# Layer norm of the second token block: two one-element steps on ScalarE instead of GpSimd, with a remade instruction order

## The chip, the cores and the metric

The kernel runs on one core of one Trainium2 chip. Its engines work at the same time and meet only at semaphores: TensorE (PE, matmuls), VectorE (DVE), ScalarE (ACT), GpSimd (POOL), and SyncE (SP), which here issues nearly all DMA transfers. The metric is the device time of one execution in microseconds (us). "Before" is the median of four runs.

## The reference

A two-layer MLP over 2048 tokens behind a layer norm without learned scale or shift. Everything arrives and leaves in bfloat16.

```python
B, S, D, F = 1, 2048, 1024, 3584
def _layernorm(x, axis=-1, eps=1e-5):
    m = jnp.mean(x, axis=axis, keepdims=True)
    v = jnp.var(x, axis=axis, keepdims=True)
    return (x - m) / jnp.sqrt(v + eps)

def reference(x, w1, b1, w2, b2):
    y = _layernorm(x, axis=-1)
    h = _gelu(jnp.einsum("bsd,df->bsf", y, w1) + b1)
    return jnp.einsum("bsf,fd->bsd", h, w2) + b2
```

`_gelu` is the tanh approximation.

## The kernel before, in words

**Blocks and products.** The tokens are worked in two blocks of 1024 (`NSB` = 2, `s` = 0 and 1), each of eight tiles of 128. For each block the kernel normalises the tiles, forms the first product and the Gelu (`mm1_unit`, `mm1_group`, `mm1_plain`), then the second product (`mm2_block`). Both products are cut in two along each dimension and done in seven half-size products instead of eight, with additions before and after them; some of these halves are cut once more (`inner`, `mm1_group`). So PE needs fewer matmuls, and VectorE has many sums to make: sums of operands in SBUF (line 854 and others), and sums of a PSUM bank and a saved copy of it (`plus`, recorded at line 942, and lines 807 and 821). ScalarE copies PSUM banks to other banks or to SBUF (lines 780 and 962) and does the Gelus (line 792). A product that accumulates on such a copy can't start before the copy is done.

**Block 0's head.** The first tiles of x are loaded, normalised with statistics on VectorE or ScalarE (`ln`, `ln_act`), transposed on PE (line 504), and multiplied as soon as they are there (`mm1_plain`, line 619). Meanwhile PE runs 26 matmuls on ones (line 400). The bias b1 comes as rows and is transposed by one small matmul (`b1t`, line 406); its copy `b1c` is read by every Gelu.

**Block 1's layer norm.** It is `ln_act2`, line 464, and runs during block 0: three tiles (6, 7, 3) while block 0's first product runs, and five (0, 1, 2, 4, 5) while its second product does. For a tile ScalarE sums x into an accumulator (`sum`, line 469), scales the sum to the negative mean (`nm`, line 472), and squares x with that mean as bias into another accumulator (`sq`, line 474). GpSimd then makes variance plus epsilon (`vpe`, line 482), raises it to the power -1/2 (`rstd`, line 485), and multiplies negative mean and `rstd` for the bias (`nb`, line 488). Last, ScalarE writes the normalised tile as `x * rstd + nb` (`y`, line 491). Two transposing transfers per tile (`dma_T`, line 520) bring it into the layout of the first product. `vpe`, `rstd` and `nb` have one element per partition.

**What sets the order.** Each operation is given to a planner (`Planner`) with its engine, an assumed duration, the operations it depends on and a priority. The planner plays the engines forward in time and takes, on each, among those that can start soonest the one of smallest priority; the result is each engine's fixed instruction order. `ORDER` is a table that shifts the priorities of named operations. `LAT` and `PE_LAT` are assumed delays between engines. `_emit` writes each engine's instructions in that order and puts a semaphore wait ahead of an instruction for each dependence not yet known as met. This includes an engine's own earlier instructions, except for PE, which is given no wait for itself. An engine works strictly in its order: a waiting instruction holds all that stand behind it, and so does a waiting transfer on SP's queue.

**Buffers of the second product.** Within `last_block`, the four sums of an inner product on its left side (`s1` to `s4` in `inner`) go to buffers used again two products later. `war_of` lists what must be done before such a buffer is written anew: the matmuls that read it (`subs`), and stores that read it. That `s2` reads `s1`, and `s4` reads `s2`, on the same engine, is not in the list. `o22` at the end of `last_block` is made in two VectorE sums.

Of the kernel before, what the change touches and what calls it, by code (L numbers as in the profile page):

```python
# [5 lines left out]
ACT = mybir.ActivationFunctionType  # L6
ALU = mybir.AluOpType
BF16 = mybir.dt.bfloat16
FP16 = mybir.dt.float16
F32 = mybir.dt.float32  # L10
# [12 lines left out]
LN_EPS = 1e-5  # L23
P = 128
# [12 lines left out]
DMA_T = (5, 6, 7)  # L37

ORDER = {n: float(x) for n, x in (e.split(":") for e in """
    G1_5g_0_5:5.5 G1_5g_1_5:8.8 G2_5g_0_3:-15.8 G2_5g_1_3:0.8 G3_5g_0_3:7.3 G3_5g_0_5:-4.7 G3_5g_1_1:-25.3  # L40
    G4_5g_1_1:13 G6_5g_0_5:-21 G7_5g_0_3:9.2 G7_5g_0_5:6.5 M11_1:8.3 M15_0:17 M24_0:-3.1 M27_1:5.7 M43_0:-8.5
    M47_0:7.7 M51_1:7.2 M57_0:16.8 M6_0_0:3.3 M72_1:-20.2 O12_0_1:11.2 O12_0_3:8.4 P1_0_6:10.3 P1_0_9:-1.1
    P1_1_2:-2.7 P1_1_3:-18.7 P1_1_6:0.2 P2_0_12:-1 P2_0_5:0.7 P3_0_10:-9.9 P3_0_11:5.1 P3_0_12:-7.3 P3_0_2:-10.3
    P3_1_6:9.8 P4_0_3:7.4 P4_0_9:-17.7 P4_1_0:40.5 P4_1_1:54.4 P4_1_3:2 P6_0_12:-3.6 P6_0_4:1.1 P6_1_11:4.1
    P7_0_6:-33.7 c7_0_11:2.3 c7_0_5:1.2 c7_0_8:-5.5 c7_0_9:8.4 c7_1_12:9.1 c7_1_13:1.2 g12_1_1:13.1 g12_1_3:2.2
    g21_1_8:25.8 g22_0_2:1.3 g22_0_3:1.6 gS0_5g_1_3:20 gS1_5g_0_3:-6.6 gS1_5g_0_5:11.2 gS3_5g_0_5:14.9 g_0_3_2:-14.6
    hS2_0_1:-7.5 hS3_1_0:8.3 hS4_0_1:-4.8 hS4_0_3:39 iS3_1_1_0:41 iS3_2_0_0:8.3 iS5_3_1_0:28.6 iS5_4_0_0:-14.1
    iS5_5_0_0:-10 iS6_5_0_0:-3.7 iT4_1_0_0:4.1 iT4_2_0_0:3.8 iT4_3_0_0:13.3 iT5_3_0_0:14.2 iT6_1_0_0:4.6
    iT6_2_0_0:1.3 iT6_4_0_0:6.6 iT6_5_0_0:-8.9 k5_3_1:16.7 k5_5g_0_5:35.6 o12_3_0:-17 pT1_2:-34.8 pT1_3:15 pT1_6:4.8
    pT2_1:1.7 pT2_2:7.7 pT3_3:10.8 pT3_5:-2.2 pT4_0:-7.2 pT4_3:-4.3 pT4_4:-7 pT4_5:-2.4 pT4_6:7.9 plain_0_7_2None:35  # L50
    plain_0_7_3None:8.5 pw2_0:-4.4 r11_5g_1_5:-18.2 r12_5_0:10.8 r22_1_0:14.3 r22_5g_0_3:33.7 s2_2_0:-7.2
    sd1_0_2:11.5 sn1_0_9:12.1 sn1_1_10:2.8 sn1_1_5:-0.5 sn5_0_4:-29.1 st0_5_0:-3.9 w1T13_1_0:3.4 w1T1_0_4:30.1
    w1T1_0_6:-5.1 w1T1_1_2:3.5 w1T2_1_1:26.1 w1T3_0_6:-17.7 w1T4_1_3:15 w1_0_0_1:9.9 w1_0_3_0:-7.9 w1_0_5_0:-24
    w1_0_5_1:-0.6 w1_1_0_0:0.7 w1_1_6_1:-1.9 w6_0_11:-4.1 w6_0_5:-9.5 w6_1_5:-44.2 wi5_3:20.8 x0_0_1:-11.2 x1_0:4.8
    y1_6:-8.5 yS1_1_0:6.2 yS2_0_0:8.2 yS2_1_0:-3.4 yS4_1_0:8.6 yi13_1:14.5 yi2_0:-15 yt0_6_0:-2.3
""".split())}

MM512 = 0.2159
MM256 = 0.1092
MM128 = 0.0562  # L60
LAT = 0.12
PE_LAT = 0.2
DMA_RATE = 0.35e6
DMA_RATE0 = 0.29e6
# [41 lines left out]
class Planner:  # L106
# [8 lines left out]
    def add(self, *a, **k):  # L115
        o = Op(*a, **k)
        o.prio += ORDER.get(o.name, 0.0)
        self.ops.append(o)
        return o
# [29 lines left out]
    def place(self):  # L149
        free = {e: 0.0 for e in self.ENGS}  # L150
# [11 lines left out]
        while left:  # L162
# [32 lines left out]
                o.deps += list(dict.fromkeys(rel for rel in rels if rel is not None))  # L195
                h.pool.free = [f for f in h.pool.free if not k <= f[0] < k + h.n]
            c = o.cost[e] if isinstance(o.cost, dict) else o.cost
            free[e] = r + c
            if o.nbytes is not None:
                dma_free = max(dma_free, r + c)  # L200
                dma_free += o.nbytes / (DMA_RATE0 if dma_free < 4.0 else DMA_RATE)
# [57 lines left out]
def bass_standalone__mixer_channel_mlp__prompt_kernel(  # L259
# [24 lines left out]
    with ExitStack() as es:  # L284
# [18 lines left out]
        identb = sb("identb", [P, P], BF16)  # L303
        ones = sb("ones", [P, P], FP16)
        nhalf = sb("nhalf", [P, 1], F32)
        st_sb = sb("st_sb", [P, NT, 12], F32)
        mv_sb = sb("mv_sb", [P, NT, 2], F32)
        vpe_sb = sb("vpe_sb", [P, NT], F32)
# [59 lines left out]
        def load_w1(s, c, prio, gate=(), eng="SP"):  # L368
# [11 lines left out]
                                                           compare_op=ALU.is_equal, fill=0.0, base=0,  # L380
                                                           channel_multiplier=1), (c_ones,), -7, "identb")
        c_nh = add("POOL", 0.1, lambda e: e.memset(nhalf[:, :], -0.5), (), -8, "nhalf")

        load_x(0, 0, (), -400, halves=True, eng=("SP", "ACT"))
        load_x(0, 1, (), -390)
# [12 lines left out]
        def warm(n, deps, prio):  # L398
# [5 lines left out]
        warm(N_WARM, (), -200)  # L404
        hold_b = Holder(banks, leaves=False)
        b1t = add("PE", 0.2, [(lambda e: e.transpose(out=ps16[:, hold_b.k, 0:FT].bitcast(BF16), in_=b1r_sb[:, :],
                                                    identity=identb[0:FT, 0:FT]), ())], (c_idb, b1_ld), 11.0, "b1t",
                  alloc=hold_b)
        b1c = add("ACT", 0.2, lambda e: e.copy(out=b1_sb[:, :], in_=ps16[:, hold_b.k, 0:FT].bitcast(BF16)), (b1t,), 12.0,
                  "b1c", frees=(hold_b,))  # L410
# [53 lines left out]
        def ln_act2(s, i, prio, war=None):  # L464


            junk = junk1 if war is None else junk2
            war = [*(war or ()), *junk_last[-1:]]
            a0 = add("ACT", 1.25, lambda e: e.activation(out=junk, in_=x_sb[:, i, :].rearrange("p (a c) -> p a c", a=2), func=ACT.Identity,  # L469
                                                         accum_out=mv_sb[:, i, 0:1]), [*x_ld[(s, i)], *war], prio,  # L470
                     f"sum{s}_{i}")
            a1 = add("ACT", 0.2, lambda e: e.mul(mv_sb[:, i, 1:2], mv_sb[:, i, 0:1], -1.0 / D), (a0,), prio + 0.001,
                     f"nm{s}_{i}")
            a2 = add("ACT", 1.35, lambda e: e.activation(out=junk, in_=x_sb[:, i, :].rearrange("p (a c) -> p a c", a=2), func=ACT.Square,  # L474
                                                         bias=mv_sb[:, i, 1:2], scale=1.0,
                                                         accum_out=st_sb[:, i, 0:1]), (a1,), prio + 0.002,
                     f"sq{s}_{i}")
            junk_last.append(a2)
            if junk is junk1:
                for u in (NU - 2, NU - 1):  # L480
                    h_head.setdefault((22, u), []).append(a2)
            vp = add("POOL", 0.2, lambda e: e.tensor_scalar(out=vpe_sb[:, i:i + 1], in0=st_sb[:, i, 0:1],
                                                           scalar1=1.0 / D, scalar2=LN_EPS, op0=ALU.mult, op1=ALU.add),
                     (a2,), prio + 0.003, f"vpe{s}_{i}")
            rs = add("POOL", 0.6, lambda e: e.tensor_tensor(out=rstd_sb[:, i:i + 1], in0=vpe_sb[:, i:i + 1],
                                                            in1=nhalf[:, :], op=ALU.pow), (vp, c_nh), prio + 0.004,
                     f"rstd{s}_{i}")
            nb = add("POOL", 0.3, lambda e: e.tensor_tensor(out=st_sb[:, i, 1:2], in0=mv_sb[:, i, 1:2],  # L488
                                                            in1=rstd_sb[:, i:i + 1], op=ALU.mult), (rs, a1), prio + 0.005,
                     f"nb{s}_{i}")  # L490
            y_ok[(s, i)] = add("ACT", 1.3, lambda e: e.activation(  # L491
                out=x16[:, i, :], in_=x_sb[:, i, :], func=ACT.Identity, scale=rstd_sb[:, i:i + 1],
                bias=st_sb[:, i, 1:2]), (nb, rs), prio + (0.006 if war is not None else 6.0), f"y{s}_{i}")
# [112 lines left out]
        def mm1_plain(c, prio):  # L606
# [3 lines left out]
            for b in range(2):  # L610
                hold = [Holder(banks) for _ in range(4)]
                done = {f: [] for f in range(4)}
                for i in range(b * TH, (b + 1) * TH):
                    t = i % TH
                    y = y_in[(0, i)]
                    for j, f in ([(j, f) for j in range(2) for f in range(4)] if i == 0 else
# [4 lines left out]
                            rhs=yop[f"A{b + 1}{k // KH + 1}"][:, k % KH, t * P:(t + 1) * P],  # L621
                            start=(k == t == 0), stop=(k == KD - 1), skip_group_check=True),
                            (ld[k // KH], y[k // KH])) for k in ks]
                        o = add("PE", len(ks) * MM128, fn, list(dict.fromkeys([*done[f][:1]] + [d for _, dd in fn for d in dd])),
                                prio[i] + 0.01 * f + 0.1 * (j or 0), f"plain_{c}_{i}_{f}{j}",
                                alloc=hold[f] if t == 0 and not j else None)
                        w1_use[c].append(o)
# [301 lines left out]
        def mm2_block(s, W):  # L929
# [8 lines left out]
            kept = {p: [] for p in SEQ2}  # L938
            stores = []
            last_ = {}  # L940
            done = lambda p: users[p]
            plus = lambda e, out, x, y: e.tensor_tensor(out=out, in0=x, in1=y, op=ALU.add)  # L942

# [92 lines left out]
            def inner(p, a, Yo, xb, war, O=None, bias=None, out=None, gate=(), ogate=(), kk=None, tmp=None, tail=False):  # L1036
# [19 lines left out]
                    Holder(banks, seeded=bias is not None)  # L1056
                bank = {1: c0, 6: c0, 7: c0, 4: c0, 2: c2, 5: c5, 3: c5}
                subs, ev = {}, {}

                def sub(r, deps, alloc=None):  # L1060
                    x, y = opn[r]
# [122 lines left out]
            def last_block():  # L1184
# [39 lines left out]
                def give(names, subs):  # L1224
                    for r, b in zip(SEQ1, names):
                        use[b] = [subs[r]]
# [38 lines left out]

                gw, okq, sub7 = inner(7, S3, Yo[7], XX, war_of(sub2), O=(g1, O12), kk=dl_sb[:, :], gate=(sub5[5],))
                give(hold[7], sub7)
                for i in range(2):
                    ho = Holder(outs, 2)
                    q = 10 * i + 11  # L1270
                    rows = lambda g, i=i: sn_sb[:, g.k + 2 * i:g.k + 2 * i + 2, :].rearrange(
                        "p j (v c) -> p v j c", v=2)
                    f = [add("DVE", 1.22, lambda e, i=i, ho=ho, rows=rows: plus(
                        e, o_sb[:, ho.k:ho.k + 2, :].rearrange("p v (j c) -> p v j c", j=2), rows(gw), rows(g5)),
                        (okq[q], okq[q + 1], *O12.values()), pt[7] + 7 * SUB + 0.1 * i, f"o22_{s}_{i}", alloc=ho,
                        frees=(g5,) if i else ())]
                    store(22, 2 * i, 2, ho, f, pt[7] + 7 * SUB)

# [2 lines left out]
                      tail=True)  # L1281

            def war_of(subs, p=None):
                return {(c, r): [subs[r]] + ([ti_st[p][r]] if c == "T" and r in ti_st.get(p, {}) else [])
                        for c in "ST" for r in subs}

            if s + 1 == NSB:
# [225 lines left out]
```

## Time and profile before

| what | us |
|---|---|
| median of four runs | 338.58 (338.35 to 339.25) |
| the profiled execution's own time | 338.51 |
| its span, first to last instruction | 336.8 |
| PE busy | 330.4 |
| VectorE busy | 281.6 |
| ScalarE busy | 173.4 |
| GpSimd busy | 22.3 |
| ScalarE waiting for GpSimd's `nb` (line 488), 4 times | 6.7 |

The span leaves out what lies before the first and after the last instruction. Matmuls are pipelined: a matmul's recorded length is longer than the distance to the next start, and rows of busy time hide gaps that are shorter than that difference. The distance between starts is the better measure. An engine's idle time costs nothing unless something on the path that ends last waits for it. GpSimd's lengths include the time in which it waits for SBUF.

### The profile page before, as it was taken

How to read it: one execution, taken by the hardware profiler on the slowest of the kernel's cores; microseconds unless marked ns; L12 is line 12 of the kernel's file. 1: busy time of each engine (PE TensorE's matmuls, PEld its weight loads, DVE VectorE, ACT ScalarE, POOL GpSimd, SP SyncE). 2: the span in 40 equal slices, each digit the busy share in tenths (PEclk: the TensorE clock that was granted, in tenths of full speed). 3: DMA queues.
4: the chain of work that ended last, by engine and by line, in shares of the span. 5: the costliest groups of instructions: out<-in, count | busy, mean ns of one | idle time of the engine just before them, and what ended most of it. 6: DMA issues, size and time to landing. Idle time of an engine off the chain costs nothing.

```text
span 336.8 us, 6035 instructions
## 1 busy us (share of the span) xinstructions
PE 330.4 (98%) x2399; PEld 224.2 (67%) x2399; DVE 281.6 (84%) x381; ACT 173.4 (52%) x292; POOL 22.3 (7%) x47
## 2 busy tenths in 40 slices
PE   5999999999999999999999999999999999999996
PEld 4977445445468885547875555544545888888885
DVE  3986789998999989979999978886738879999984
ACT  5675878566876687612113666765675521010200
POOL 2320120000020413200000000000000000000000
PEclk9999999999999999999999999999999999999999
DMA  7896999797879999899859549839972999998103
GB/s 220 281 204 164 357 364 307 262 305 255 270 279 275 362 356 360 221 295 373 345 174 313 185 187 333 291 130 293 350 233 54 385 313 365 333 366 274 64 0 127
DMA packets 80310, 89.47 MB, mean 266 GB/s; under 512 B 15130, under 2 KB 67226, under 8 KB 79770
## 3 DMA queue, kind: packets, MB, share of 16 engines
q1 hardware_dynamic: 80138, 88.95, 81.8%
q8 instruction: 19, 0.31, 0.4%
q10 hardware_dynamic: 144, 0.13, 0.1%
q14 instruction: 9, 0.07, 0.1%
HBM read 61.81 MB, written 24.38 MB: 256 GB/s over the span
## 4 chain that ended last, share of the span: by engine, by line
PE 93%; ACT 3%; DMA 2%; POOL 1%; issue 0%; SPq 0%; DVE 0%
PE ps L767 42%; PE ps L1063 34%; PE ps L978 7%; PE ps L619 5%; PE ps L692 5%; DMA w_sb<-in_w_dram 2%; POOL st_sb L488 1%; ACT t_sb L474 1%; PE ps L504 1%; ACT t_sb L469 1%; PE ps L1068 0%; ACT sn_sb L962 0%; ACT ps L962 0%; ACT x_sb L491 0%; SPq L350 0%
## 5 line engine op out<-in xcount | busy, mean ns | idle before, releaser
L767 PE MATMUL ps<-yw_sb,t_sb 128*128 128x512 f16 x336 | 80.0, 379 | 0.0
L767 PE MATMUL ps<-yw_sb,w_sb 128*128 128x512 f16 x312 | 74.7, 379 | 0.0
L792 ACT ACTIVATE h_sb<-ps,b_sb 128x512 f16<-128x512 f32 x78 | 52.9, 687 | 37.0 <-PE ps L767 32.3
L767 PEld LDWEIGHTS ps<-yw_sb,t_sb 128*128 128x128 f16 x336 | 32.7, 98 | 35.9 <-DVE ps L807 0.5
L767 PEld LDWEIGHTS ps<-yw_sb,w_sb 128*128 128x128 bf16 x312 | 30.3, 98 | 33.2 <-ACT ps L780 0.3
L854 DVE TENSOR_TENSOR h_sb<-h_sb 128x2048 f16<-128x2048 f16 (+2 forms) x36 | 38.6, 1085 | 7.3 <-ACT h_sb L792 5.3
L962 ACT COPY sn_sb<-ps 128x512 f32<-128x512 f32 x27 | 15.5, 584 | 32.9 <-DVE o_sb L942 18.2
L1063 PE MATMUL ps<-w2a_sb,h_sb 128*128 128x256 f16 (+1 forms) x252 | 30.3, 273 | 0.0
L942 DVE TENSOR_TENSOR sn_sb<-ps,sn_sb 128x512 f32<-128x512 f32 x35 | 24.0, 688 | 5.3 <-PE ps L1063 4.5
L1063 PEld LDWEIGHTS ps<-w2a_sb,h_sb 128*128 128x128 f16 x252 | 24.7, 98 | 3.9
L942 DVE TENSOR_TENSOR o_sb<-ps,sn_sb 128x512 bf16<-128x512 f32 (+1 forms) x29 | 19.3, 670 | 6.3 <-PE ps L1063 3.7
L978 PE MATMUL ps<-w2a_sb,h_sb 128*128 128x512 f16 x112 | 24.5, 379 | 0.0
L1063 PE MATMUL ps<-w_sb,t_sb 128*128 128x256 f16 x196 | 23.4, 273 | 0.1
L962 ACT COPY ps<-sn_sb 128x512 f32<-128x512 f32 x12 | 7.1, 589 | 30.3 <-PE ps L1063 24.6
L780 ACT COPY ps<-ps 128x512 f32<-128x512 f32 x26 | 14.9, 577 | 14.5 <-PE ps L767 14.5
L1063 PEld LDWEIGHTS ps<-w_sb,t_sb 128*128 128x128 f16 x196 | 19.0, 98 | 2.7 <-ACT sn_sb L962 0.4
L807 DVE TENSOR_TENSOR ps<-ps,sn_sb 128x512 f32<-128x512 f32 x26 | 17.7, 695 | 3.5 <-PE ps L767 3.4
L587 DVE TENSOR_TENSOR t_sb<-w_sb,t_sb 128x1024 f16<-128x1024 bf16 x26 | 17.9, 688 | 3.2 <-DMA w_sb<-in_w_dram 2.0
L792 ACT ACTIVATE h_sb<-sn_sb,b_sb 128x512 f16<-128x512 f32 x26 | 18.5, 717 | 3.7 <-DVE sn_sb L821 2.8
L978 PEld LDWEIGHTS ps<-w2a_sb,h_sb 128*128 128x128 f16 x112 | 11.0, 98 | 12.8
L619 PE MATMUL ps<-yw_sb,w_sb 128*128 128x128 f16 x256 | 17.4, 231 | 0.3 <-DMA w_sb<-in_w_dram 0.3
L821 DVE TENSOR_TENSOR sn_sb<-ps,sn_sb 128x512 f32<-128x512 f32 x20 | 13.6, 688 | 4.5 <-PE ps L767 4.4
(125 smaller groups left out, 486.8 us busy)
## 6 DMA issues: line engine op xcount, KB each, us to landing
w_sb<-in_w_dram SPq DMA_DIRECT2D x28, 512.0 KB, 5.9
x_sb<-in_w_dram SPq DMA_DIRECT2D x21, 256.0 KB, 6.2
w_sums<-x_sb SPq DMA_DIRECT2D x21, 256.0 KB, 3.5
w2a_sb<-w_inner_sums SPq DMA_DIRECT2D x12, 448.0 KB, 7.2
x_sb<-in_x_dram SPq DMA_DIRECT2D x15, 256.0 KB, 6.1
w_inner_sums<-w_sb SPq DMA_DIRECT2D x4, 896.0 KB, 8.7
x_sb<-w_sums SPq DMA_DIRECT2D x2, 1792.0 KB, 8.9
w_sb<-w_inner_sums SPq DMA_DIRECT2D x8, 448.0 KB, 7.2
```

Of the source, the lines that this page charges most:

```text
L587: return add("DVE", 0.65, lambda e: e.tensor_tensor(out=tv(k), in0=x0, in1=x1, op=ALU.subtract), [*deps, *war.get(k, ())], prio + 0.5 * k, ...
L619: fn = [(lambda e, b=b, hb=hold[f], f=f, k=k, t=t: e.matmul(ps[:, hb.k, t * P:(t + 1) * P], lhsT=lhs[:, k, f * P:(f + 1) * P], rhs=yop[f"A ...
L692: fn = [(lambda e, k=k, v=v: e.matmul(ps[:, bank[r].k, v * QN:(v + 1) * QN], lhsT=xo()[:, k, v * P:(v + 1) * P], rhs=yv()[:, k, :], start= ...
L767: fn = [(lambda e, k=k: e.matmul(ps[:, hold[p].k, :], lhsT=lhs[:, k, :], rhs=yop[yo][:, k, :], start=(first and k == 0), stop=(k == KH - 1 ...
L780: return e.copy(out=dst, in_=src) if o_.eng == "ACT" else e.tensor_copy(dst, src)
L792: r = h_ok[(s, q, u)] = add("ACT", 0.70, lambda e: e.activation(out=dst, in_=src(), func=ACT.Gelu_apprx_tanh, bias=b1_sb[:, f:f + 1], scal ...
L807: o2 = add("DVE", 0.7, lambda e: e.tensor_tensor(out=b5v(b5), in0=b5v(b0), in1=v5(), op=ALU.add), (P6, *o5), pt[7] - SLOT, f"w6_{nm}", all ...
L854: o = add("DVE", cost2(w * dst.shape[-1]), lambda e, k0=k0, k1=k1: e.tensor_tensor(out=dst[:, k0:k1, :], in0=a[0][:, k0:k1, :], in1=b[0][: ...
L942: plus = lambda e, out, x, y: e.tensor_tensor(out=out, in0=x, in1=y, op=ALU.add)
L962: return act(lambda e: e.copy(out=out(), in_=src()), deps, at - 5, name, **k)
L978: fn = [(lambda e, k=k, t=t: e.matmul(ps[:, banks_[t].k, :], lhsT=a[0][:, k, t * P:(t + 1) * P], rhs=b[0][:, k, :], start=(first and k == ...
L1063: fn = [(lambda e, k=k, j=j: e.matmul(ps[:, bank[r].k, j * HI:(j + 1) * HI], lhsT=x[0][:, k, j * P:(j + 1) * P], rhs=y[0][:, k, :], start= ...
```

## The change

In `ln_act2`, `vpe` becomes a ScalarE activation (Identity, scale 1/D, bias from a new one-column tile `epsc` that holds epsilon), and `nb` becomes a ScalarE multiply with a per-partition scale. `rstd` stays on GpSimd, now planned at 2.0 us instead of 0.6. For the three early tiles `nb` gets a priority 6 higher. A GpSimd memset fills `epsc`.

The planner subtracts 0.08 us from each VectorE and 0.09 us from each ScalarE operation when it works out when the engine is free (`OVL`). The bias transpose `b1t` moves from priority 11 to -92, and the plain products of the second half of the tiles depend on it. `war_of` now also lists the left-side sums that read `s1` and `s2`, and the second `o22` sum depends on the first. The table `ORDER` is remade: some entries stay, many are dropped, changed or new. Of it only a few lines are shown.

```diff
 ORDER = {n: float(x) for n, x in (e.split(":") for e in """
-    G1_5g_0_5:5.5 G1_5g_1_5:8.8 G2_5g_0_3:-15.8 G2_5g_1_3:0.8 G3_5g_0_3:7.3 G3_5g_0_5:-4.7 G3_5g_1_1:-25.3
+    G1_5g_0_5:5.5 G1_5g_1_3:2 G1_5g_1_5:-3 G2_5g_0_3:-15.8 G2_5g_1_3:4.3 G2_5g_1_5:-2.9 G3_5g_0_3:8.5
...
-    y1_6:-8.5 yS1_1_0:6.2 yS2_0_0:8.2 yS2_1_0:-3.4 yS4_1_0:8.6 yi13_1:14.5 yi2_0:-15 yt0_6_0:-2.3
+    yS1_1_0:3.6 yS2_0_0:8.2 yS4_1_0:9.1 yi13_1:15.1 yi2_1:-4.4 yi4_1:-1.5
 """.split())}
...
+OVL = {"DVE": 0.08, "ACT": 0.09}
...
-            free[e] = r + c
+            free[e] = r + c - OVL.get(e, 0.0)
...
+        epsc = sb("epsc", [P, 1], F32)
...
+        c_eps = add("POOL", 0.1, lambda e: e.memset(epsc[:, :], LN_EPS), (), -6, "eps")
...
-                                                    identity=identb[0:FT, 0:FT]), ())], (c_idb, b1_ld), 11.0, "b1t",
+                                                    identity=identb[0:FT, 0:FT]), ())], (c_idb, b1_ld), -92.0, "b1t",
...
-            vp = add("POOL", 0.2, lambda e: e.tensor_scalar(out=vpe_sb[:, i:i + 1], in0=st_sb[:, i, 0:1],
-                                                           scalar1=1.0 / D, scalar2=LN_EPS, op0=ALU.mult, op1=ALU.add),
-                     (a2,), prio + 0.003, f"vpe{s}_{i}")
-            rs = add("POOL", 0.6, lambda e: e.tensor_tensor(out=rstd_sb[:, i:i + 1], in0=vpe_sb[:, i:i + 1],
+            vp = add("ACT", 0.2, lambda e: e.activation(out=vpe_sb[:, i:i + 1], in_=st_sb[:, i, 0:1], func=ACT.Identity,
+                                                        bias=epsc[:, :], scale=1.0 / D), (a2, c_eps), prio + 0.003,
+                     f"vpe{s}_{i}")
+            rs = add("POOL", 2.0, lambda e: e.tensor_tensor(out=rstd_sb[:, i:i + 1], in0=vpe_sb[:, i:i + 1],
                                                             in1=nhalf[:, :], op=ALU.pow), (vp, c_nh), prio + 0.004,
                      f"rstd{s}_{i}")
-            nb = add("POOL", 0.3, lambda e: e.tensor_tensor(out=st_sb[:, i, 1:2], in0=mv_sb[:, i, 1:2],
-                                                            in1=rstd_sb[:, i:i + 1], op=ALU.mult), (rs, a1), prio + 0.005,
-                     f"nb{s}_{i}")
+            nb = add("ACT", 0.2, lambda e: e.mul(st_sb[:, i, 1:2], mv_sb[:, i, 1:2], rstd_sb[:, i:i + 1]), (rs, a1),
+                     prio + (0.005 if war is not None else 6.0), f"nb{s}_{i}")
...
-                        o = add("PE", len(ks) * MM128, fn, list(dict.fromkeys([*done[f][:1]] + [d for _, dd in fn for d in dd])),
+                        o = add("PE", len(ks) * MM128, fn, list(dict.fromkeys([*done[f][:1], *([b1t] if b else [])] + [d for _, dd in fn for d in dd])),
...
+            s_read = {}
...
+                s_read[id(subs)] = {5: s2[1][0], 6: s4[1][0]}
...
+                f = []
...
-                        (okq[q], okq[q + 1], *O12.values()), pt[7] + 7 * SUB + 0.1 * i, f"o22_{s}_{i}", alloc=ho,
+                        (okq[q], okq[q + 1], *O12.values(), *f), pt[7] + 7 * SUB + 0.1 * i, f"o22_{s}_{i}", alloc=ho,
...
-                return {(c, r): [subs[r]] + ([ti_st[p][r]] if c == "T" and r in ti_st.get(p, {}) else [])
+                return {(c, r): [subs[r]] + ([ti_st[p][r]] if c == "T" and r in ti_st.get(p, {}) else []) + (
+                    s_read[id(subs)].get(r, []) if c == "S" else [])
```

More of the change, by code (lines that the diff above doesn't have):

```diff
@@ L39 @@
 ORDER = {n: float(x) for n, x in (e.split(":") for e in """
-    G1_5g_0_5:5.5 G1_5g_1_5:8.8 G2_5g_0_3:-15.8 G2_5g_1_3:0.8 G3_5g_0_3:7.3 G3_5g_0_5:-4.7 G3_5g_1_1:-25.3
-    G4_5g_1_1:13 G6_5g_0_5:-21 G7_5g_0_3:9.2 G7_5g_0_5:6.5 M11_1:8.3 M15_0:17 M24_0:-3.1 M27_1:5.7 M43_0:-8.5
-    M47_0:7.7 M51_1:7.2 M57_0:16.8 M6_0_0:3.3 M72_1:-20.2 O12_0_1:11.2 O12_0_3:8.4 P1_0_6:10.3 P1_0_9:-1.1
-    P1_1_2:-2.7 P1_1_3:-18.7 P1_1_6:0.2 P2_0_12:-1 P2_0_5:0.7 P3_0_10:-9.9 P3_0_11:5.1 P3_0_12:-7.3 P3_0_2:-10.3
@@ L44 @@
[L44 to L53, printed above, removed]
@@ L54 @@
-    w1_0_5_1:-0.6 w1_1_0_0:0.7 w1_1_6_1:-1.9 w6_0_11:-4.1 w6_0_5:-9.5 w6_1_5:-44.2 wi5_3:20.8 x0_0_1:-11.2 x1_0:4.8
-    y1_6:-8.5 yS1_1_0:6.2 yS2_0_0:8.2 yS2_1_0:-3.4 yS4_1_0:8.6 yi13_1:14.5 yi2_0:-15 yt0_6_0:-2.3
+    G1_5g_0_5:5.5 G1_5g_1_3:2 G1_5g_1_5:-3 G2_5g_0_3:-15.8 G2_5g_1_3:4.3 G2_5g_1_5:-2.9 G3_5g_0_3:8.5
+    G3_5g_1_1:-37.6 G5_5g_0_3:5.9 G7_5g_0_3:9.2 M11_1:7 M12_1:-22 M23_0:-5.1 M27_1:5.7 M35_0:-3.3 M42_0:-4.6
+    M45_0:16.6 M47_0:7.7 M47_1:-10.4 M51_1:7.2 M52_1:-3.3 M57_0:16.8 M72_1:-20.2 P1_0_6:-3.7 P1_0_9:-1.1 P1_1_2:-4
@@ new lines @@
+    P1_1_3:-25.5 P1_1_9:-0.9 P2_0_8:9 P2_0_9:1.3 P2_1_6:6.6 P2_1_9:4.5 P3_0_11:5.1 P3_0_12:-7.3 P3_0_2:-2.5
+    P3_0_6:-18.5 P3_1_1:-7 P3_1_3:12.1 P3_1_5:2.1 P3_1_6:9.8 P3_1_7:0.4 P4_0_3:7.3 P4_0_4:2.4 P4_0_7:5.1 P4_1_0:29.5
+    P4_1_1:54.9 P6_0_13:3.3 P6_0_8:-3.6 P6_1_9:-7.6 P7_0_6:-34.1 P7_0_9:-5.2 P7_1_4:2.7 c7_0_8:-32.2 c7_0_9:7.5
+    c7_1_12:9.1 c7_1_2:21.7 c7_1_3:-7.4 g22_1_1:-37.4 g22_1_4:-5.7 gS1_5g_0_3:-17.2 gS3_5g_0_5:17.1 gS3_5g_1_1:-0.3
+    hS2_0_2:-4.4 iS3_2_0_0:9.2 iS5_3_1_0:28.6 iT4_3_0_0:13.3 iT57_4_0:-17.9 iT57_5_0:-10.6 iT6_1_0_0:4.6
@@ new lines @@
+    iT6_3_0_0:1.5 k5_3_1:16.7 pT1_3:31.6 pT2_1:-33.5 pT2_2:7.5 pT2_3:7.7 pT3_3:11.5 pT3_5:4.4 pT3_6:-4.5 pT4_0:-16.5
+    pT4_4:-6.6 pT4_6:8.9 plain_0_7_2None:35 pw2_0:-6.6 r22_1_0:23.5 sn1_0_12:3.7 sn1_1_7:-6.2 sn1_1_8:-2.4
+    sn5_0_4:-29.1 st0_4_1:11.2 tI7_3:32.2 tl6:-16.4 w1T13_1_0:-15.3 w1T1_0_4:29.4 w1T2_1_1:17.3 w1T3_0_6:-16.9
+    w1T4_1_0:15.9 w1_0_0_1:9.9 w1_0_5_0:-24 w1_1_2_0:0.4 w1_1_4_1:-36.8 w1_1_6_1:-4.8 w2_0_B22_1:2 w6_0_6:1.7
+    w6_0_7:7.6 w6_1_0:-2.9 w6_1_3:20.1 w6_1_4:-0.3 w6_1_5:-47.2 x0_0_1:-11.2 x1_0:4.8 y0_1:14.5 y1_6:-8.5
```

## The prediction

> **What bounds the kernel now.** I read the share table first. In these rows each engine has its busy time, its share of the span and its instructions.
>
> ```profile
> span 336.8 us, 6035 instructions
> PE 330.4 (98%) x2399; PEld 224.2 (67%) x2399; DVE 281.6 (84%) x381; ACT 173.4 (52%) x292; POOL 22.3 (7%) x47
> PEclk9999999999999999999999999999999999999999
> ```
>
> TensorE (PE) has work for 98% of the span at full clock, and the change touches none of its 2399 matmuls. The question is only how much idle time is in the other 2%, and whether the change can reach it. The chain that ended last, in order of time (start, length, what), shows where PE is not the releaser:
>
> ```profile
> 1.73 5.91 DMA w_sb<-in_w_dram
> 7.69 1.89 PE ps L619 x16
> ...
> 19.95 1.79 PE ps L619 x32
> ...
> 113.09 0.76 POOL vpe_sb L482
> ...
> 114.54 2.83 POOL st_sb L488
> 117.38 0.03 issue
> 117.40 1.24 ACT x_sb L491
> ...
> 122.54 4.76 PE ps L1063 x42
> ...
> 154.53 18.34 PE ps L1063 x168
> ...
> 332.70 1.54 PE ps L1068 x14
> 334.25 0.02 issue
> 334.27 0.42 DVE o_sb L942
> ```
>
> Up to 7.69 the first weights arrive; from 334.25 the last sum and store run out (2.5 us); between, PE. At 108.7 to 122.5 the chain wanders over ScalarE and GpSimd (ACT and POOL), 13.8 us long. That is not 13.8 us of stall: the table by stretches has PE busy for 14.00 of the 14.00 us from 108 to 122. The timeline tells what was lost. Columns: start, length, engine, line, operation.
>
> ```profile
> 114.30 2.02 DVE L1022 TENSOR_TENSOR w_sb<-yw_sb 128x3584 f16<-128x3584 bf16 x1
> 114.54 2.82 POOL L488 TENSOR_TENSOR st_sb<-mv_sb,rstd_sb 128x1 f32<-128x1 f32 x1
> 116.23 1.09 DVE L854 TENSOR_TENSOR t_sb<-h_sb 128x1792 f16<-128x1792 f16 x1
> 117.40 1.24 ACT L491 ACTIVATE x_sb<-x_sb,st_sb,rstd_sb 128x1024 f16<-128x1024 bf16 x1 [2.00 <-POOL st_sb L488]
> 118.55 0.56 ACT L962 COPY sn_sb<-ps 128x512 f32<-128x512 f32 x1
> 121.92 0.56 ACT L962 COPY sn_sb<-ps 128x512 f32<-128x512 f32 x1
> 122.53 1.42 PEld L1063 LDWEIGHTS ps<-w_sb,t_sb 128*128 128x128 f16 x14 [0.40 <-ACT sn_sb L962]
> ```
>
> A one-element GpSimd multiply took 2.82 us, until two VectorE (DVE) sums had ended. ScalarE stood 2.00 us before the normalising activation, so everything behind it in ScalarE's order came late. The PSUM copy that ended at 122.48 held PE: the matmul starts around it are 0.395 us apart where 0.109 is usual, so 0.286 us were lost. It is the only such gap between 12 and 334 us.
>
> Matmul starts give the rest. From 7.69 on, spacing above the usual is 2.51 us in all: 0.286 here; 0.191 and 0.106 in the head, around the bias transpose at 9.51; 1.77 is early 128-column matmuls spaced 0.107 instead of 0.056; the last 0.15 is scatter.
>
> **What the Trainium skill says.** "GPSIMD Engine Reference", section "Key points": GpSimd contends for SBUF with a VectorE instruction that has two SBUF inputs. The trace agrees: L488 took 0.19 us with a PSUM-reading sum beside it, and 2.82, 1.23, 1.05 and 1.02 us beside two-SBUF-input sums. "ScalarE: Activation LUTs", section "What ACT_TABLE_LOAD costs": an ACTIVATE costs 186 ns, plus 93 for each per-partition pointer operand, and back-to-back ones overlap by 93 ns. The trace has 200 ns for the 128x1 one without pointers (L472), and copies of 0.56 to 0.59 us start 0.48 us apart. "TensorE: Matmul & The Clock Gate", section "Part 1: The HAM clock gate": a cold array runs at half clock until it has been busy for one free-running window. That fits the 0.107 spacing up to 12.07 us, which this edit cannot shorten by design, though its end can move between executions.
>
> **The change part by part.**
>
> *Removed from GpSimd.* Eight variance steps (L482, 3.0 us in all, mean 372 ns) and eight bias steps (L488, 7.2 us, mean 897). ScalarE waited 6.7 us in four stalls for the latter. What of that is on PE's path is the 0.286 us.
>
> *Added to ScalarE.* Eight variance activations with one pointer (the epsilon column) and eight multiplies scaled by a pointer. No such row exists with pointers; nearest is L472 at 0.200, and the skill's price is 0.28. I take 0.28, bounds 0.20 and 0.37. Then 16 x 0.28 = 4.5 us, 5 x 0.56 = 2.8 of it between 108 and 142 us, where the stalls saved were four, 6.7 us. ScalarE is busy 10.42 of 14 us from 108 to 122 and 14.43 of 23 from 122 to 145; 3.6 and 8.6 us are free, so the extra is hidden if the order keeps it out from before a copy that PE waits for. Uncovered, one pair is 0.56 us against copy margins down to 0.09 us: the copy that starts at 118.55 ends at 119.11, and the matmul that needs it starts at 119.20. That would be a stall of about 0.5 us.
>
> *The chain of one tile.* Before, worst case: square ends 113.00, normalising starts 117.40, 4.4 us. After: variance 0.28 + hop 0.07 + power 0.56 + hop 0.06 + bias 0.28 + 0.03 = 1.3 us plus whatever holds the power.
>
> *The power that stays.* L485 took 0.55 us in seven of eight cases, because the variance step ahead of it absorbed the hold (0.74, 0.70, 0.45, 0.32 us where 0.19 is free). It will now be first at the port. Holds seen on a first step average 0.18 us; on any step the longest is 2.82 - 0.19 = 2.63. I take 0.2 to 0.5, bounds 0 and 2.63. The order table assumes 2.0 us for it, so up to 1.45 us of hold has other ScalarE work planned over it.
>
> *Transposes.* The normalised tiles leave by two transposing transfers each on SP's queue (118.67 and 120.85 for this tile). They are unchanged in number but become free up to 2 us sooner; behind them in that queue stand loads of w2 sums, which can only be released earlier by it. Worth nothing on PE, whose gaps here are not transfers.
>
> *Epsilon memset.* One more on GpSimd, 0.10 us like L382, at about 1.65 us; the engine is idle from there to 5.18. Free.
>
> *Bias transpose.* Its priority rises, and second-half plain matmuls name it as an earlier step on PE, for which PE emits no wait. It already ran at 9.51, when nothing else was ready. I take 0 with bounds -0.3 (both head gaps close) and +0.3.
>
> *Own-engine order.* New waits on VectorE for its own earlier work: the next sums' buffers wait for sums several instructions back, met long ago; the second of two closing sums waits for the first, losing an overlap of about 0.08 us (sums of 0.69 start 0.61 apart). VectorE is busy 28.06 of 30 us from 290 to 320, but these come where PE is several products ahead. 0, upper bound 0.3.
>
> *The order table.* The largest unknown. Every engine's order is made anew, with VectorE and ScalarE operations counted 0.08 and 0.09 shorter, which are the overlaps the trace shows. The old order leaves PE one gap in 322 us. A new one can hardly do better, and any product put before its copy or sum is late costs a gap: margins at PE's waits, from the end of the copy or sum to the matmul that needs it, start at 0.09 us, and many are 0.6 to 0.8. I take +0.1, bounds 0 and +3 (several sums late by one 0.69 us place).
>
> Sum for the likeliest: -0.286 + 0 + 0 + 0.1 = -0.2 us. The profiled execution took 338.51 (span 336.8, 1.7 around it), the median 338.58, 0.07 more. So 338.51 - 0.2 + 0.07 = 338.4.
>
> The floor follows too. With all of 0.286, 0.191, 0.106 and the scatter of 0.15 gone the gain is 0.73 us, 337.85. Only a half-clock phase that ends sooner goes below: 1.77 us at the very most.
>
> **The rivals.** *A: no measurable change, 338.4*, as summed. For it: one matmul order is as dense as another once operands are in time. Against: new orders rarely meet every margin.
>
> *B: slower, the new order opens gaps in PE, 339.6.* Mechanism: a VectorE sum that is read by the next product (L807 and L942 in the two matrix products) takes a place behind an operand sum of 1.09 us. VectorE has only 16% free, so it cannot catch up at once. With a usual margin of 0.64 us each such place costs 1.09 - 0.08 - 0.64 = 0.37 us; four give 1.5, less 0.29 saved: 338.58 + 1.2 = 339.8, three give 339.4. It decides from three places on. Against: the durations assumed now fit the trace better than before.
>
> *C: slower by the power's hold, 339.3.* At a tile whose power meets two long sums (2.63 us, as L488 did), ScalarE stands at the bias step 1.2 us past the plan, and the PSUM copy behind it has 0.09 to 0.8 us of margin: 0.4 to 1.1 us a time. Two such tiles near 1.0 less 0.29 give 339.3; one alone stays within A. Against: the first-step holds seen end at 0.55 us.
>
> *D: faster, 337.7.* The gap at 122.5 and the head's gaps close, and the half-clock phase ends a little sooner. For it: four holds of GpSimd go. Against: only 0.73 us is there without the clock.
>
> That the change doesn't do what it says is unlikely: its functions are Identity and a scaled copy, and Identity (L469) already runs between Gelus with a single table load in the whole profile.
>
> **How the numbers follow.** A 0.46, B 0.28, C 0.09, D 0.17. 0.2% of 338.58 is 0.68 us, about what a measurement of this kernel can tell from no change; so A lies within, B and C above 339.26, D below 337.90: faster 0.17, same 0.46, slower 0.37. A's own range is 337.9 to 339.2. For 8 in 10, D's best third is left out below and the upper third of B above: 337.6 to 340.6.
>
> **What would show it.** Right: L482 and the bias line appear on ScalarE near 0.2 to 0.3 us each; GpSimd keeps only L485 in block 1, with one or two held above 1 us; ScalarE's 6.7 us of waits for GpSimd shrink to under 3; PE's start gap at 122.5 is gone; the head to 7.69 and the tail of 2.5 us stay. A wrong forecast would show as start gaps on PE over 0.3 us: beside a late VectorE sum it is B, beside a copy behind the bias step C. A head whose half-clock spacing ends elsewhere than 12 us would mean the clock, not the edit, moved the time.

## The result, and the profile after

The changed kernel takes 340.06 us in the median (338.69 to 346.50, 33 executions), the kernel before 338.63 (337.46 to 340.28, 52). The ratio is 1.0048, with a 95% interval of 1.0036 to 1.0059: about 1.6 us slower. (The ratios leave out disturbed executions, so they are not exactly the quotients of the medians.)

The profiled execution hides this. It took 338.69 us, the fastest of all 33, and its span, 336.9 us, is that of the execution profiled before (336.8). First the share table:

```profile
span 336.9 us, 6019 instructions
PE 329.9 (98%) x2399; PEld 223.6 (66%) x2399; DVE 278.7 (83%) x380; ACT 178.0 (53%) x309; POOL 15.0 (4%) x32
```

The groups of the moved steps (busy and mean length; then the idle time before them):

```profile
L483 ACT ACTIVATE vpe_sb<-st_sb,epsc 128x1 f32<-128x1 f32 x8 | 2.3, 292 | 0.2
L486 POOL TENSOR_TENSOR rstd_sb<-vpe_sb,nhalf 128x1 f32<-128x1 f32 x8 | 6.9, 864 | 112.6 <-ACT vpe_sb L483 112.6
L489 ACT ACTIVATE st_sb<-mv_sb,rstd_sb 128x1 f32<-128x1 f32 x8 | 2.3, 289 | 1.6 <-POOL rstd_sb L486 1.6
```

The move did what it says. The two steps cost 0.29 us each on ScalarE; GpSimd has 7.3 us less work; ScalarE waits 1.6 us for GpSimd instead of 6.7. The power now takes the wait that GpSimd's first step has beside VectorE's sums: 0.86 us in the mean instead of 0.57. The gap of 0.286 us at 122.5 us is gone.

But PE has new gaps, in the head. From PE's timeline of the changed kernel (idle time and releaser in brackets; the recorded length hides part of a gap):

```profile
16.85 0.62 PE L504 MATMUL ps<-ident,x_sb 128*128 128x128 f16 x8 [0.26 <-DVE x_sb L430]
23.08 1.89 PE L767 MATMUL ps<-yw_sb,w_sb 128*128 128x512 f16 x8
25.21 1.99 PE L619 MATMUL ps<-yw_sb,w_sb 128*128 128x128 f16 x28 [0.24 <-DMA yw_sb<-x_sb]
```

By the distance between starts, 0.42 us are lost at 16.85, where tile 4's normalising (L430) is late, and 0.40 and 0.24 us at 25.21 and 25.68, where the plain products of tile 6 wait for its two transposed halves.

The first of these is no late load: tile 4 had landed at 10.01. In the remade order its normalising stands on VectorE behind tile 5's and behind a sum of weights (L587), and it waits for a GpSimd power that took 0.86 us beside that sum, where the one before it took 0.57:

```profile
15.10 0.69 DVE L587 TENSOR_TENSOR t_sb<-w_sb 128x1024 f16<-128x1024 bf16 x1
15.35 0.86 POOL L427 TENSOR_TENSOR rstd_sb<-vpe_sb,nhalf 128x1 f32<-128x1 f32 x1
16.25 0.55 DVE L430 TENSOR_SCALAR x_sb<-x_sb,mv_sb,rstd_sb 128x1024 f16<-128x1024 bf16 x1 [0.46 <-POOL rstd_sb L427]
```

For the gaps of tile 6, SP's queue shows what stands in front of its transposes. Before:

```profile
16.11 0.93 SPq L350 DMA_DIRECT2D w_sb<-in_w_dram  x2
17.42 8.39 SPq L520 DMA_TRANSPOSE yw_sb<-x_sb  x6
```

After:

```profile
15.21 2.62 SPq L520 DMA_TRANSPOSE yw_sb<-x_sb  x2
17.88 1.14 SPq L350 DMA_DIRECT2D w_sb<-in_w_dram  x2
19.47 5.88 SPq L520 DMA_TRANSPOSE yw_sb<-x_sb  x4
```

A megabyte of weights now stands between tile 5's and tile 6's transposes. It landed at 24.68 us, tile 6's halves at 25.16 and 25.64. Before, PE came to tile 6 only at 26.81, 2.0 us after the second half had landed.

From PE's first transpose on, start gaps over 0.07 us add up to 1.89 us, 1.80 of them before 26 us; before it was 1.13. That is 0.76 more. But the early half-clock spacing (0.107 us between matmuls of 128 columns instead of 0.056) ended sooner, at 11.07 us against 12.21 (the prediction read 12.07), so it and the scatter came to 1.69 us instead of 2.43, which is 0.74 less. The two cancel, and the span is nearly the same. The half-clock phase ended anywhere from 9.5 to 14.6 us in the profiles that follow.

### The profile page after: what moved, and what is told of

It reads as the page before. It is cut to its first block, busy times and chain, and to the rows that moved or that the text cites. A ratio compares the mean times of both kernels' runs of the same rounds, so it can differ in the third digit from the quotient of the medians.

```text
span 336.9 us, 6019 instructions
## 1 busy us (share of the span) xinstructions
PE 329.9 (98%) x2399; PEld 223.6 (66%) x2399; DVE 278.7 (83%) x380; ACT 178.0 (53%) x309; POOL 15.0 (4%) x32
## 4 chain that ended last, share of the span: by engine, by line
PE 92%; DVE 4%; DMA 2%; POOL 1%; issue 0%; SPq 0%; DVEq 0%
PE ps L767 41%; PE ps L1065 38%; PE ps L979 7%; PE ps L692 5%; DVE st_sb L419 2%; DMA yw_sb<-x_sb 1%; PE ps L619 1%; DMA x_sb<-in_x_dram 1%; DVE x_sb L430 1%; POOL rstd_sb L427 1%; PE ps L1070 0%; DVE mv_sb L423 0%; DVE x_sb L453 0%; DVE yw_sb L511 0%; POOL vpe_sb L424 0%
## 5 line engine op out<-in xcount | busy, mean ns | idle before, releaser
L767 PEld LDWEIGHTS ps<-yw_sb,w_sb 128*128 128x128 bf16 x312 | 30.4, 98 | 33.1
L943 DVE TENSOR_TENSOR sn_sb<-ps,sn_sb 128x512 f32<-128x512 f32 x35 | 23.8, 686 | 1.5 <-PE ps L1065 1.4
L587 DVE TENSOR_TENSOR t_sb<-w_sb,t_sb 128x1024 f16<-128x1024 bf16 x26 | 17.8, 684 | 3.4 <-PE ps L767 2.3
L619 PEld LDWEIGHTS ps<-yw_sb,w_sb 128*128 128x128 bf16 x256 | 15.7, 102 | 2.0 <-DMA yw_sb<-x_sb 1.0
```

Of the source, the lines that this page charges most:

```text
L587: return add("DVE", 0.65, lambda e: e.tensor_tensor(out=tv(k), in0=x0, in1=x1, op=ALU.subtract), [*deps, *war.get(k, ())], prio + 0.5 * k, ...
L619: fn = [(lambda e, b=b, hb=hold[f], f=f, k=k, t=t: e.matmul(ps[:, hb.k, t * P:(t + 1) * P], lhsT=lhs[:, k, f * P:(f + 1) * P], rhs=yop[f"A ...
L767: fn = [(lambda e, k=k: e.matmul(ps[:, hold[p].k, :], lhsT=lhs[:, k, :], rhs=yop[yo][:, k, :], start=(first and k == 0), stop=(k == KH - 1 ...
```

## The experiments

After the result there were two theories, not to be mixed up with the prediction's rivals A to D: **theory A**, the remade order costs the time (in the head, or in the body, which here means all after 30 us), and **theory B**, the two steps on ScalarE cost it. A start gap is the amount by which the distance between two matmul starts exceeds the usual one.

| kernel | median us | ratio to before | 95% interval |
|---|---|---|---|
| changed, again | 340.16 | 1.0048 | 1.0029 to 1.0068 |
| changed, again | 340.28 | 1.0044 | 1.0016 to 1.0072 |
| new order, steps on GpSimd | 340.97 | 1.0069 | 1.0037 to 1.0100 |
| kernel before, steps on ScalarE | 338.24 | 0.9989 | 0.9973 to 1.0004 |
| all of the change but the order | 338.52 | 0.9984 | 0.9971 to 0.9996 |
| the same, again | 338.34 | 0.9987 | 0.9974 to 0.9999 |
| old head, new rest | 339.19 | 1.0014 | 0.9992 to 1.0036 |
| the same, again | 339.55 | 1.0019 | 1.0003 to 1.0035 |
| new head, old rest | 340.74 | 1.0059 | 1.0037 to 1.0081 |
| old to 95 us, new after | 339.23 | 1.0011 | 0.9997 to 1.0025 |
| new from 30 to 95 us only | 339.74 | 1.0026 | 1.0008 to 1.0043 |

**Order against operations.** The first two experiments take the steps and the order apart. In one, the changed kernel keeps its order and the steps go back to GpSimd around the power:

```diff
         order = pl.place()
+        for o in [o for o in order["ACT"] if o.name.startswith(("vpe1_", "nb1_"))]:
+            order["ACT"].remove(o)
+            o.eng = "POOL"
+            k = next(k for k, r in enumerate(order["POOL"]) if r.name == "rstd" + o.name[-3:])
+            order["POOL"].insert(k + (o.name[0] == "n"), o)
```

> The changed kernel with the variance and bias steps back on GpSimd, around the power; the order of all else is as it was. Theory A: the loss stays, 339.7 to 341 us, since the head is untouched; a little may come on top between 108 and 142 us, where GpSimd's holds return. Theory B: 338.3 to 338.9 us, as before the change.

Measured 340.97, as theory A has it. In the other, the kernel before gets the steps on ScalarE, in the same way, with its order kept:

> The kernel before with only the two steps moved to ScalarE, the variance step right behind the square and the bias step right ahead of the normalising; nothing else reordered. Theory A: 338.2 to 338.6 us, 0 to 0.3 less than before, with the gap at 122.5 us gone. Theory B: 339.5 to 340.5 us.

Measured 338.24, and PE has no start gap over 0.07 us after 9.73 us. The third takes all of the change, its waits, the bias transpose's dependence and the epsilon tile, but replays the order before, engine by engine, from lists of names:

```diff
-                    if e not in o.engs:
+                    if at[e] == len(LISTS[e]) or o.name != LISTS[e][at[e]]:
                         continue
...
             o.eng = e
+            at[e] += 1
```

> The changed kernel, its own-engine waits and bias-transpose dependence included, but with every engine's order taken name by name from the kernel before (the variance step right behind the square, the bias step right ahead of the normalising). If the remade order alone costs the time: 338.1 to 338.6 us. If the own-engine waits or the epsilon memset cost something: 339.3 or more.

Measured 338.52, and in a later run 338.34:

> The change without the reordering, again, as the base of the three others and for a closer figure: 338.2 to 338.6 us, 0.1 to 0.2 per cent less than the kernel before, VectorE's waits for transfers 0.5 to 1.0 us.

So theory B is out. All of the change but its order is 0.13% faster than before (interval 0.01 to 0.26%), which is 0.4 us. With the moved steps alone (0.9989), from which it can't be told apart, it is the fastest version here. PE's timeline of that last run, where the gap at 122.5 us was:

```profile
117.76 1.69 PE L1178 MATMUL ps<-yw_sb,h_sb 128*128 128x256 bf16 x14
119.29 4.75 PE L1178 MATMUL ps<-w_sb,t_sb 128*128 128x256 f16 x42
123.88 1.69 PE L1178 MATMUL ps<-o_sb,h_sb 128*128 128x256 f16 x14
```

No line carries an idle time: 42 matmuls start one behind another, 0.109 us apart. The order alone costs 1.0048 / 0.9987, or 0.61%, 2.1 us. (The two ratios are of separate series, each against the kernel before.)

**The changed kernel again,** for executions nearer the median:

> The changed kernel once more, for a second execution's profile and as the base of the comparisons. Theory A (the loss is in the remade order of the head): 339.5 to 340.5 us; where the head's loads land later than in the first profile (the last x tile after 15.5 us instead of 14.97), the plain products of tiles 5 and 6 wait for their transposed halves, and the start gaps between 16 and 28 us add up to more than 1.5 us (1.06 in the first profile). Theory B (the two steps on ScalarE cost the time): the gaps lie between 94 and 145 us, next to ScalarE copies.

> The changed kernel once more, for the profile of an execution near its median (340 us). Theory head: the start gaps on PE before 28 us are 1.5 to 2.5 us in all and those after 30 us under 0.3. Theory body: over 0.8 us after 30 us.

The profiles missed the median again. The first is of an execution of 350.80 us, the longest of its 13, and is not used. The second is of 342.99 us, the longest of its 8. Its head gaps, without the two that both kernels have (first weights, bias transpose), are 1.42 us; but 2.60 us are lost after 30 us, so in this execution both halves of theory A hold. The waits of VectorE from 30 to 95 us in it (total, times, longest):

```profile
DVE w2a_sb L888 <- DMA x_sb<-in_w_dram: 3.4, 2, 2.4
DVE t_sb L576 <- DMA w_sb<-in_w_dram: 2.4, 2, 1.3
DVE t_sb L587 <- DMA w_sb<-in_w_dram: 0.8, 1, 0.8
```

In the run of all but the order, the same stretch has one such wait (its lines count 113 higher, so L700 is L587):

```profile
DVE t_sb L700 <- DMA w_sb<-in_w_dram: 0.6, 1, 0.6
```

What such a wait does, in the 342.99 us execution. First VectorE waits for a load, then a PE product waits for a VectorE sum that stands behind it:

```profile
91.41 0.69 DVE L888 TENSOR_TENSOR w2a_sb<-x_sb,w2a_sb 128x1024 f16<-128x1024 bf16 x1 [2.39 <-DMA x_sb<-in_w_dram]
...
95.42 1.04 PE L767 MATMUL ps<-yw_sb,w_sb 128*128 128x512 f16 x4 [0.46 <-DVE ps L807]
```

The same through ScalarE: the statistics of x tile 0 wait for its load, the copies behind them come late, then a VectorE sum, then PE:

```profile
116.52 1.06 ACT L470 ACTIVATE t_sb<-x_sb 128x1024 f16<-128x1024 bf16 x1 [2.77 <-DMA x_sb<-in_x_dram]
...
119.41 1.05 ACT L963 COPY sn_sb<-ps 128x512 f32<-128x512 f32 x2
...
123.43 1.70 PE L1065 MATMUL ps<-w_sb,h_sb 128*128 128x256 f16 x14 [1.14 <-DVE sn_sb L943]
```

By starts these are gaps of 0.62 and 1.30 us. In the first profile neither was there: VectorE's waits for loads from 30 to 95 us were 2.1 us in all, ScalarE had none for x, and PE did not feel them.

**Head against body.** Two replays join the orders at 30 us: old head with new rest, and new head with old rest. Such a join has a seam: an instruction of one order may wait there for one that the other order makes later.

> As that, but the old order only for the 167 operations of the head (up to the last plain product, about 30 us) and the remade order for all that follows. Theory head (the loss is the remade order's waits for the first tiles and transposes before 28 us): 338.1 to 338.9 us. Theory body (thin margins of VectorE and ScalarE in the remade order after 30 us lose it in most executions, though not in the one first profiled): 339.5 to 340.5 us, with start gaps of more than 0.8 us in all after 30 us.

> The other half: the remade order for the 163 operations of the head, the old order for all that follows. Theory head: 339.6 to 340.6 us, gaps before 28 us of 1.0 to 2.0 us. Theory body: 338.3 to 339.0 us.

The old head gives 0.3% back, 339.19 and, again, 339.55. The new head with the old rest stays at 340.74 (6 executions); 0.82 us of that, in its profile, is the seam, where a product at 31.92 waits for a copy that the new head makes later. So the head costs about 1 us of the 2.1 and the rest the other 1, by the old head; by the new head, less the seam, the head's part is nearer 1.6. Neither the theory of the head nor that of the body was right alone.

The profiles of all runs, each of one execution, agree with this, those of the runs below included. Not counted are the 350.80 us one, the gaps for the first weights and the bias transpose, and the seam at 31.92. PE's gaps are those over 0.07 us.

| us | old order there | remade order there |
|---|---|---|
| PE's gaps from 8 to 28 us | 0 to 0.11 in six profiles; 0.48, 0.77, 1.00 in three | 1.06 to 1.81 in eight |
| VectorE waiting for loads, 30 to 95 us | 0 to 2.1 in six | 2.0 to 7.5 in eleven |
| PE's gaps from 30 to 97 us | 0 in five, 0.44 in one | 0 in the three that waited under 4 us; 0.08 to 1.61 in the eight above |
| ScalarE waiting for x tile 0, near 112 to 117 us | 0 in six | 0 to 1.5 in eight; 2.0, 2.2, 2.8 in three, which alone have a PE gap near 122 us (0.56, 0.71, 1.30) |

The remade head loses time in every execution profiled, the remade body only where loads came late. The old head is not free of it: in three profiles its plain products also waited, for weights or transposes.

**Local repairs.** Three tries to name single instructions in the head, and one in the body. In the first, the weights stand ahead of tile 5's transposes on SP's queue, as before:

```diff
+        for n in (0, 1):
+            o = next(o for o in order["SP"] if o.name == f"w1_0_2_{n}")
+            order["SP"].remove(o)
+            order["SP"].insert(next(k for k, r in enumerate(order["SP"]) if r.name == "yt0_5_0"), o)
```

> The changed kernel with one change on SP's queue: the two loads of the third weight column block stand ahead of the transposes of tile 5, as before the change, and not between those of tiles 5 and 6. Theory A in the narrow form (the megabyte of weights in front of tile 6's transposes is the cause): 338.4 to 339.2 us, tile 6's second half lands near 24.8 us or earlier, and tile 5's later than 19.1. Theory A in the wide form (the order of the products on PE has too little between the transposes and their use): 339.5 to 340.5, the wait moves from tile 6 to tile 5. Theory B: no change.

340.88, ratio 1.0063 (1.0042 to 1.0083), above both ranges expected. Tile 6's halves landed at 24.68 and 26.06 and PE didn't wait for them; yet nothing was won, so the narrow form falls. In its profile, of the longest of 6 executions, PE waits elsewhere in the head:

```profile
10.56 1.03 PE L504 MATMUL ps<-ident,x_sb 128*128 128x128 f16 x8 [0.61 <-DVE x_sb L453]
...
19.16 0.62 PE L504 MATMUL ps<-ident,x_sb 128*128 128x128 f16 x8 [0.26 <-DVE x_sb L430]
```

Tile 1's normalising (L453) stands behind both statistics of tile 2, and so waits for that tile's load. The gap at 19.16 is that of tile 4's normalising again. Then three moves in the head:

```diff
+        move("DVE", "y0_1", ahead_of="st0_2_1")
+        move("DVE", "w1T1_0_1", behind="y0_4")
+        move("PE", "P2_0_3", ahead_of="plain_0_6_0None")
```

> The changed kernel with three moves in the head: tile 1's normalising ahead of tile 2's second statistics on VectorE, the first weight sum behind tile 4's normalising on VectorE, and one 512-column product ahead of tile 6's plain products on PE. If these three waits are the head's loss: 339.0 to 339.5 us, gaps before 28 us under 0.6 us beside the one for the first weights. If the head loses by its place as a whole: 339.9 or more.

339.77, ratio 1.0025 (1.0008 to 1.0043): about half came back. Its profile doesn't show why: the head's gaps are 1.53 us in all, no less than without the moves. Tile 4's gap fell from 0.42 to 0.24, but waits also moved on (0.75 us to tile 2's transposes at 11.61). And the store of the fifth product's sums, moved on SP's queue, with the old head, alone, and with the three moves:

```diff
+        move("SP", "is5_0", behind="yt1_3_1")
```

> The kernel with the old head and the remade rest, and one store (0.92 MB of operand sums of the fifth product) put back behind the second-product loads of block 1's x tiles on SP's queue, where the kernel before has it. If the rest's loss comes from x tile 0 landing late behind that store, so that ScalarE's statistics hold the PSUM copies behind them: 338.3 to 338.8 us, no start gap at the fourth product of the first inner block (near 122 us), and fewer executions above 340. If not: 339.0 to 339.5.

> The changed kernel with that store moved and nothing else: only the body's part comes back, 339.4 to 339.9 us, and the head's gaps of 1.1 to 1.5 us before 28 us stay. If the store has nothing to do with it: 340.0 to 340.4.

> All four moves together on the changed kernel. If head and body are understood: 338.4 to 338.9 us, no slower than before; otherwise 339.2 or more.

339.66, 341.20 and 340.54; ratios 1.0021, 1.0069 and 1.0034. The first two are above both ranges expected. Nothing was won, and the theory of that one store falls. In the first of the three the gap near 122 us was absent, as it is in five profiles of the remade body with the store where it was, and PE waited 0.82 us at the next place for a load of w2 sums:

```profile
129.39 1.68 PE L1093 MATMUL ps<-w2a_sb,h_sb 128*128 128x512 f16 x7 [0.66 <-DMA w2a_sb<-w_sums]
```

**Which part of the body.** The last two replays join the orders at 95 us, with the old head in both.

> The changed kernel with the old order for everything up to about 95 us (block 0's first product and the preparation of w2 beside it) and the remade order for all that follows. Theory transfers (in the remade order VectorE's sums between 30 and 95 us are placed right where their loads were planned to land, and every late load costs PE a gap): as all-but-order, 338.3 to 338.8 us, VectorE's waits for transfers between 30 and 95 us about 0.5 to 1.0 us. Theory second product: 339.2 to 340 us, gaps after 95 us.

> The old order for the head and from 95 us on, the remade order only between 30 and 95 us. Theory transfers: 339.1 to 340.2 us (0.9 of it can be a seam at 95 us, where both orders meet), VectorE's waits for transfers there 2 to 7 us. Theory second product: 338.3 to 338.9 us.

> Old head, remade rest, again, on the chip of the two others: 339.0 to 339.7 us as before; VectorE's waits for transfers between 30 and 95 us 4 to 7 us. Theory transfers: its distance to all-but-order is the same as that of the order new from 30 to 95 us.

New between 30 and 95 us gives 1.0026, new after 95 us 1.0011, against 0.9987 for old throughout: 1.3 and 0.8 us, together nearly twice the 1.1 of the whole rest (1.0019). So the seams cost something too: in the profile of new after 95 us, gaps of 0.17 and 0.50 at 99.8 and 105.1 us are in no other run. The first stretch seems to have the larger share, but the intervals overlap. VectorE's waits for transfers there were 5.4 us with the stretch new and 2.1 with it old (0.5 to 1.0 was expected), 6.8 with old head and new rest.

A reading of the single executions goes with it. All but the order ran from 337.50 to 339.68 in 22 executions, old head with new rest from 337.22 to 341.46, new from 30 to 95 us from 337.56 to 342.06. The best ones are the same; the new order has a longer upper end. That fits the table: the remade body is not looser work, it is less tolerant of late transfers. The head's part is different. With it even the fastest of the 33 executions, 338.69, is 1.2 us above the fastest before, 337.46.

The two orders' own plans tell part of why. The planner works out when each load lands. The sum `pT1_6`, whose wait of 2.39 us is shown above, was planned 3.87 us after its load's landing before, and 0.12 us after it (`LAT`, the least possible) in the remade order; `pT1_0` went from 0.49 to 0.12, `pT1_5` from 0.31 to 0.12. Of all uses of loads planned between 30 and 95 us, two stood at that least distance before and eight do now. The load of `pT1_6` landed at 91.39 in the 342.99 us execution, 4.11 us after its issue. The plans don't tell why ScalarE now waits for x tile 0, whose statistics stand 0.12 us after the landing in both.

## Why the prediction was wrong

The likeliest case was rival A, no measurable change at 338.4; the time is 340.06. It lies in the range of 337.6 to 340.6 only because that took in part of rival B. Point by point:

- **Removed from GpSimd: right.** The 0.286 us gap went, in the changed kernel and in every replay with the old order. Without the reordering the change gains 0.4 us (0.13%, interval 0.01 to 0.26%), against the 0.29 forecast.
- **Added to ScalarE: right.** 0.292 and 0.289 us against 0.28 taken.
- **The power: about right.** It took 0.31 us over its 0.55 in the mean (0.86) where 0.2 to 0.5 was taken; the longest was 1.44. In the execution of 342.99 us it was more, 0.58, with a longest of 2.17. No PE gap behind a bias step was found, so rival C didn't happen.
- **Epsilon memset, own-engine waits, bias transpose: zero as far as the medians tell.** With the old order, the kernel with all of them (0.9984, 0.9987) and the one with the moved steps alone (0.9989) agree; the gap at the bias transpose is 0.19 us in both orders. But the four profiles of these edits with the old order after 95 us have a PE gap of 0.23 to 0.33 us at 197 to 199 us, behind a VectorE sum that waits for weights; the kernel before and the one with the moved steps alone don't. The weights took 6.13 to 6.24 us to land there instead of 5.83 and 5.89. Why is open.
- **The order table: this is the step that failed.** It was given +0.1 us, with +3 as its bound; it measures +2.1. I argued that the old order left PE one gap, and that durations nearer to the trace speak for the new one. Both hold, but neither says what the new order puts in front of what. It put tile 4's normalising behind a sum of weights (0.42 us), tile 6's transposes behind a megabyte of weights (0.64 us in the first profile), and sums onto the landing of their loads. The margins I listed on PE's waits were those to copies and sums; how long before its use each load had landed, on VectorE and ScalarE as well, was never read.
- **"PE, whose gaps here are not transfers"** was not quite true of the order before. The gap of 0.106 us, put down to the bias transpose, is at 10.53, ahead of the product that needs the second half of the first weights, which had landed at 10.48. And the claim was carried over to an order that I hadn't seen, in which tile 6's transposes and the late loads are transfers.
- **Rival B** had the right sign and a near time, 339.6. Its mechanism was half right. At 16.85 a VectorE step that PE needs does stand behind an operand sum, though it is a normalising in the head. In the body PE does wait for late VectorE sums, but in the two chains shown VectorE is late because it, or ScalarE, stood waiting for a load. That the time came near 339.6 is in part luck: three or four late places in the two products, on which it was worked out, were not what happened.

What stays open: how much of the head's 1 us each of its waits costs, how the body's 1 us divides at 95 us, and whether late loads are all of it. That they cost the body's time is read from profiles of single executions; no run changed the distance from landing to use alone.

## What to carry to other kernels

When a static order is remade, list for each engine how long every load lands before its first use, in the old profile, and see which of these distances the new plan gives up. Here the order that kept them had no more than one PE gap from 30 to 97 us in any profile, and the one planned onto the landings had gaps in eight of eleven. A change of operations and a change of order are worth separate measurements: here the first gained 0.4 us and the second lost 2.1. One profile of an execution at the edge of the range can show no loss at all; compare it with the list of all times before explaining it.

## What I had not expected of the hardware

The early half-clock phase of PE ended at different times in executions of one kernel: near 11 us in the changed kernel's first profile (27 matmuls 0.107 us apart) and at 12.75 us in the one of 342.99 us (45 of them). And the head's loads varied alike: the first half of the first weights landed at 6.24 us in the changed kernel's first profile and at 7.64 in the one before, though both are the third transfer on the same queue.
